# Banded attention and two gated layers on one core: the first unit's k and q at the head of the load queue, and the second batch's loads moved behind the first batch's units

## The chip, the core and the metric

The program runs on one core of one Trainium2 chip. The core has a matrix engine (PE, with its weight load PEld), a vector engine (DVE), an engine for activations and copies (ACT), a general engine (POOL) and an engine that only issues loads here (SP). The metric is the device time of one execution in microseconds, and of several executions the median.

## What is computed

Three steps in float32. First an attention over 2 batches, 8 heads, 768 positions and 64 columns a head, in which a position sees 31 neighbours and one summary row for each block of 32 positions:

```python
k_sum = k.reshape(B, H, nb, block, D).max(axis=3)
v_sum = v.reshape(B, H, nb, block, D).mean(axis=3)
scores_l = scale * np.matmul(q, k.transpose(0, 1, 3, 2))      # kept where |i - j| < 16
scores_s = scale * np.einsum('bhsd,bhnd->bhsn', q, k_sum) + np.log(block)
a = softmax(concatenate([scores_l_masked, scores_s], axis=-1))
x = np.matmul(a, np.concatenate([v, v_sum], axis=2))           # then (1536, 512)
```

Then two layers on the 1536 rows of x: `(sigmoid(x @ w_gate) * (x @ w_val)) @ w_out` with 1536 inner columns, and `max(x @ w1, x @ w2, x @ w3) @ w_out` with 768 inner columns.

## The kernel before

**Units.** The attention is cut into 16 units, one for a batch b, a pair of heads p (4 pairs) and a half of the positions a. The units run in the order b, a, p, so that units 0 to 7 are the first batch and 8 to 15 the second. `make_sums` makes, once for a batch and a pair, the block maxima of k (`ks`, on DVE, from the load `kn`) and the block means of v (`vs`; in the first batch eight matmuls on PE over the load `vn`, line 520; in the second three additions on POOL and one matmul). `make_unit` then makes a unit: scores on PE from q and k (line 590), mask and maximum on DVE (line 597), exponentials on ACT (line 603), division on DVE, transposes on PE (line 622), the product with v (line 632, the task kept in `pvs`), and the split of the result into a rounded part and a remainder (tile `x`; ACT line 348, DVE line 351). In the first batch the keys are read straight from `kn`; in the second batch each unit has a load of its own, `kw`. Each unit also loads `q` and `v`.

**Weights.** The weights arrive as 64-bit numbers, 512 KB for each 128x512 tile (`raw`, three buffers). DVE packs each into float32 in three passes (lines 405, 410 and 414), then ACT rounds it (line 348) and DVE takes the remainder (line 351) into `w`, of which there are twelve buffers. Every product is done as three matmuls of rounded parts. The first layer's products are at lines 711 and 745, the second's at 835 and 942.

**Order.** No order is written out. Every piece of work is a task with an engine, a duration, a due time and what it depends on, and `Plan.order` lays all tasks out by a list schedule with these figures. The instructions then stand in that order on each engine, and each engine works them off strictly in turn. So a load is not tied to its due time on the chip: it has a place in SP's queue, and SP issues it when its turn has come and its buffer is free. The argument `after` of a task only asks the plan to start it no sooner than another task has started; it adds no semaphore. While PE would wait early in the program, the plan fills the time with idle matmuls (line 994), as many as it expects to fit before the task's start, on the tile that the task will write.

The due times of loads are counted back from a unit's target T (`KEYS0`, `SUMS0`, `ROWS0` for the first batch; `KEYS`, `SUMS`, `ROWS` for the second) and from a weight's first use (`WLOAD`, and `WLOAD0` besides for the first ten weights). Of the loads that are ready, the one that is due first goes first.

Of the kernel before, what the change touches and what calls it, by code (L numbers as in the profile page):

```python
# [18 lines left out]
WIN = 16  # L19
# [8 lines left out]
LAST = 2  # L28
LASTACC = 12
KEYS0, KEYS = 14.0, 24.0  # L30
SUMS0, SUMS = 14.0, 8.0
ROWS0, ROWS = 2.0, 4.0
WLOAD = 24.0
WLOAD0 = 2.0
WREADY = 8.0
FREE_M = 2
BY_ACT = 6
# [6 lines left out]
BANKS_KW, BANKS_KN, BANKS_Q, BANKS_V = 2, 4, 3, 3  # L44
# [28 lines left out]
class Plan:  # L73
# [11 lines left out]
    def add(self, eng, dur, due, fn, deps=(), new=(), uses=(), after=(), tab=None):  # L85
        t = Task(eng, dur, due, fn, [d for d in deps if d], list(new), list(uses), [d for d in after if d], tab)
        self.tasks.append(t)
        return t
# [114 lines left out]
def kernel(  # L203
# [16 lines left out]
    B, NPAIR, _, S = qt.shape  # L220
    D = vw.shape[-1]
# [8 lines left out]
    TPU = HALF // 128  # L230
    CW = 96 + NB
# [55 lines left out]
    add = plan.add  # L287
# [5 lines left out]
    def psum_s(shape):  # L293
        return Buf(ps_s, shape, F32, "s", 4)
# [92 lines left out]
    def convert():  # L387
# [3 lines left out]
        def to_float(ck, t):  # L391
# [25 lines left out]
            n += 1  # L417
            l = add("SP", 1.456, t - WLOAD - WLOAD0 * (n <= 10), load, new=[r], after=[prev.get("l")])
            k1 = add("DVE", 0.335, t - 2.7, c1, [l], [c], [r], [prev.get("1")])
# [66 lines left out]
    def after(tag, t):  # L486

        p = chain.get(tag)
        if p:
            t.after.append(p)  # L490
        chain[tag] = t
        return t

    def load_task(tag, n, shape, src, dur, t):
        b = Buf(ap_, shape, F32, tag, n)

        def fn(what=tag):
            nc.sync.dma_start(out=b.t[0:src.shape[0]], in_=src)

        return b, after(tag, add("SP", dur, t, fn, new=[b]))  # L500

    kblock, vblock, pvs = {}, {}, {}
    attention = []

    def make_sums(b, p, T):

        kt, lk = load_task("kn", BANKS_KN, [128, S + 2 * WIN], kn[b, p], 1.14, T - (KEYS if b else KEYS0))
        r, lr = load_task("vn", 2, [96, 2, 8 * D], vn[b, p], 1.092, T - (SUMS if b else SUMS0))
        ks = Buf(ap_, [128, NB], F32, "ks", 4)
        vs = Buf(ap_, [128, 2 * D], F32, "vs", 4)  # L510
        ps = psum_s([128, 2 * D])

        def kmax():
            nc.vector.tensor_reduce(
                out=ks.t, in_=kt.t[:, WIN:WIN + S].rearrange("p (n w) -> p n w", w=BLK), axis=AX.X, op=ALU.max)

        def vsum():

            for n in range(8):
                nc.tensor.matmul(  # L520
                    ps.t, lhsT=avg, rhs=r.t[:, :, D * n:D * n + D], start=(n == 0), stop=(n == 7))

        def vadd():
            for n in (4, 2, 1):
                nc.gpsimd.tensor_tensor(
                    out=r.t[:, :, 0:n * D] if n > 1 else vr.t, in0=r.t[:, :, 0:n * D],
                    in1=r.t[:, :, n * D:2 * n * D], op=ALU.add)

        def vmean():
            nc.tensor.matmul(ps.t, lhsT=avg, rhs=vr.t, start=True, stop=True)  # L530

        def vcopy():
            nc.scalar.activation(out=vs.t, in_=ps.t, func=ACTF.Copy)

        k = add("DVE", 0.87, T - 13.5, kmax, [lk], [ks], [kt])
        if b == 0:
            v1, v2 = None, add("PE", 1.75, T - 5, vsum, [lr, built], [ps], [r])
        else:
            lr.after.append(pvs[4 + p])
            vr = Buf(ap_, [96, 2, D], F32, "vr", 2)  # L540
            v1 = add("POOL", 2.5, T - 8, vadd, [lr, built], [vr], [r])
            v2 = add("PE", 0.22, T - 5, vmean, [v1], [ps], [vr])
        v3 = add("ACT", 0.2, T - 4.5, vcopy, [v2], [vs], [ps])
        kblock[b, p] = ks, k, kt, lk
        vblock[b, p] = vs, v3
        attention.extend([k, v2, v3] + ([v1] if b else []))

    def make_unit(u, i):
        b, p, a = u
        T = target[u]  # L550
        if a == 0:
            make_sums(b, p, T)
        whole = b == 0
        ks, kk, kt, lk = kblock[b, p]
        if not whole:
            kt, lk = load_task("kw", BANKS_KW, [128, TPU, 2, CW], kw[b, p, a], 1.024, T - KEYS)
        q, lq = load_task("q", BANKS_Q, [128, HALF], qt[b, p, :, HALF * a:HALF * a + HALF], 0.546,
                          T - (KEYS0 if whole else KEYS))
        vt, lv = load_task("v", BANKS_V, [CW, TPU, 2, 2, D], vw[b, p, a], 0.82, T - (ROWS0 if whole else ROWS))
        vs, kv = vblock[b, p]  # L560
        e = [Buf(ap_, [128, TPU, CW], F32, f"e{h}", 2) for h in range(2)]
        nm = Buf(ap_, [128, 2, TPU], F32, "nm", 2)
# [395 lines left out]
    for i, u in enumerate(units):  # L958
        make_unit(u, i)
# [22 lines left out]
    with tc.manual_schedule():  # L982
        idle = const.tile([128, 384], BF16, name="idle")
        nc.vector.memset(idle, 0.0)
        for t in plan.order():
            for b in t.new:
                b.take()
            if t.idle:
# [3 lines left out]
                n = min(o.shape[1], 384)  # L992
# [62 lines left out]
```

## Time and profile before

| | |
|---|---|
| median of 3 runs | 565.29 us (564.71 to 569.85) |
| the profiled execution | 564.06 us, of which 562.3 us is the span from first to last instruction |
| PE busy | 543.9 us, 97% of the span |
| DVE busy | 430.7 us, 77% |
| ACT busy | 286.8 us, 51% |
| loads and stores | 71.96 MB, mean 128 GB/s over the span |

A busy PE is not PE at its peak, since its matmuls overlap and their ends are modelled. The shares are means over stages that differ: the attention of the first batch, the first layer with the second batch's attention beside it, the second layer, and the last product.

### The profile page before, as it was taken

To read this page: it belongs to the slowest core of one execution; us is meant where nothing else is said; L and a number is where in the kernel's file an instruction comes from. 1 tells how busy PE (TensorE), PEld (TensorE's weight loads), DVE (VectorE), ACT (ScalarE), POOL (GpSimd) and SP (SyncE) were. 2 spreads that over 40 slices of the span, in tenths; PEclk is the share of its full clock that TensorE was granted. 3 is DMA by queue.
4 is the path that set the end of the run, shared out by engine and by line. 5 is a ranking of instruction groups with operands and counts; after the bars stand their busy time and mean duration, and the time that the engine had idled before them with its cause. 6 is when DMAs were issued, how large, how long until landed. Compare 5 with 4: busy or idle time off the path is not lost.

```text
span 562.3 us, 10192 instructions
## 1 busy us (share of the span) xinstructions
PE 543.9 (97%) x3924; PEld 521.4 (93%) x3924; DVE 430.7 (77%) x987; ACT 286.8 (51%) x663; POOL 16.1 (3%) x30
## 2 busy tenths in 40 slices
PE   8689899999999999999999999999999999999997
PEld 7578799999999999999999999999999999997886
DVE  6789958894697598949996996799999997885000
ACT  4689776583765656966441332435344333453111
POOL 2001221100000000000000000000000000000000
PEclk9999999999999999999999999999999999999999
DMA  8999653563266453520652553120322222000111
GB/s 296 318 268 283 201 174 135 166 208 113 81 195 187 141 150 110 170 75 1 188 186 78 155 182 114 53 98 21 108 87 87 77 74 82 32 1 37 57 72 60
DMA packets 24288, 71.96 MB, mean 128 GB/s; under 512 B 2736, under 2 KB 6192, under 8 KB 24240
## 3 DMA queue, kind: packets, MB, share of 16 engines
q1 hardware_dynamic: 21120, 67.58, 38.7%
q10 hardware_dynamic: 3120, 3.74, 1.9%
q8 instruction: 31, 0.51, 0.4%
q14 instruction: 17, 0.14, 0.1%
HBM read 67.57 MB, written 3.15 MB: 126 GB/s over the span
## 4 chain that ended last, share of the span: by engine, by line
PE 81%; DVE 7%; DMA 5%; ACT 5%; issue 1%; SPq 1%; ACTq 0%; DVEq 0%
PE m L711 30%; PE m L745 16%; PE s L835 11%; PE m L835 11%; PE m L942 9%; DMA vn<-in_vn_dram 3%; PE s L632 2%; DMA raw<-in_wts_dram 1%; DVE c L414 1%; DVE c L410 1%; PE s L622 1%; ACT e L617 1%; ACT e L603 1%; DVE c L405 1%; PE s L590 1%
## 5 line engine op out<-in xcount | busy, mean ns | idle before, releaser
L711 PE MATMUL m<-x,w 128*128 128x384 f32 x1152 | 211.0, 338 | 0.5 <-ACT t L725 0.3
L711 PEld LDWEIGHTS m<-x,w 128*128 128x128 f32 x1152 | 198.7, 188 | 2.5 <-issue 0.6
L745 PE MATMUL m<-h,w 128*128 128x384 f32 x576 | 107.3, 338 | 0.7 <-DVE h L351 0.7
L745 PEld LDWEIGHTS m<-h,w 128*128 128x128 f32 x576 | 99.3, 188 | 2.0 <-DVE h L351 1.4
L348 ACT ACTIVATE w<-c 128x512 fp32r<-128x512 f32 x96 | 58.1, 610 | 71.6 <-DVE c L414 48.4
L351 DVE TENSOR_TENSOR w<-c,w 128x512 fp32r<-128x512 f32 x96 | 63.8, 665 | 12.6 <-ACT w L348 12.4
L414 DVE SCALAR_TENSOR_TENSOR c<-raw,c 128x512 int32<-128x512 int32 x96 | 66.7, 697 | 0.6
L410 DVE SCALAR_TENSOR_TENSOR c<-raw,c 128x512 int32<-128x512 int32 x96 | 66.0, 689 | 0.6
L835 PE MATMUL m<-x,w 128*128 128x384 f32 x294 | 56.3, 335 | 1.2 <-ACT t L850 1.2
L835 PE MATMUL s<-f,w 128*128 128x384 f32 x294 | 56.0, 334 | 0.0
L835 PEld LDWEIGHTS m<-x,w 128*128 128x128 f32 x294 | 51.3, 188 | 1.6 <-ACT t L850 1.5
L835 PEld LDWEIGHTS s<-f,w 128*128 128x128 f32 x294 | 51.4, 188 | 0.0
L405 DVE TENSOR_SCALAR c<-raw 128x512 int32<-128x512 int32 x96 | 41.7, 437 | 5.7 <-DMA raw<-in_wts_dram 4.7
L725 ACT ACTIVATE t<-m 128x384 f32<-128x384 f32 x48 | 23.4, 491 | 35.2 <-PE m L711 34.8
L730 DVE TENSOR_TENSOR t<-m,t 128x384 f32<-128x384 f32 x48 | 26.6, 554 | 15.3 <-PE m L711 10.8
L348 ACT ACTIVATE h<-t 128x384 fp32r<-128x384 f32 x48 | 24.9, 521 | 25.7 <-DVE t L730 23.8
L603 ACT ACTIVATE e<-e,nm 128x120 f32<-128x120 f32 x96 | 36.6, 384 | 1.3 <-DVE nm L597 1.1
L351 DVE TENSOR_TENSOR h<-t,h 128x384 fp32r<-128x384 f32 x48 | 26.9, 563 | 5.4 <-ACT h L348 5.4
L952 ACT ACTIVATE c<-m 128x512 f32<-128x512 f32 (+1 forms) x13 | 7.3, 565 | 40.0 <-PE m L942 39.6
L850 ACT ACTIVATE t<-s 128x384 f32<-128x384 f32 x27 | 13.3, 491 | 24.4 <-PE s L835 24.4
L942 PE MATMUL m<-w,x 128*128 128x512 f32 (+1 forms) x126 | 24.9, 359 | 0.0
L942 PE MATMUL m<-w,f 128*128 128x512 f32 x108 | 24.7, 389 | 0.0
(108 smaller groups left out, 586.4 us busy)
## 6 DMA issues: line engine op xcount, KB each, us to landing
raw<-in_wts_dram SPq DMA_DIRECT2D x96, 512.0 KB, 4.3
v<-in_vw_dram SPq DMA_DIRECT2D x16, 288.0 KB, 4.8
kn<-in_kn_dram SPq DMA_DIRECT2D x8, 400.0 KB
vn<-in_vn_dram SPq DMA_DIRECT2D x8, 384.0 KB
q<-in_qt_dram SPq DMA_DIRECT2D x16, 192.0 KB, 5.2
kw<-in_kw_dram SPq DMA_DIRECT2D x8, 360.0 KB, 10.0
out_dram<-c ACTq DMA_DIRECT2D x11, 256.0 KB, 2.0
v<-vs ACTq DMA_DIRECT2D x8, 72.0 KB
```

Of the source, the lines that this page charges most:

```text
L348: nc.scalar.activation(out=dst, in_=src, func=ACTF.Copy)
L351: nc.vector.tensor_tensor(out=dst, in0=src, in1=h.bitcast(F32), op=ALU.subtract)
L405: nc.vector.tensor_scalar(out=c.t, in0=half(r, 1), scalar1=5, scalar2=2, op0=ALU.logical_shift_left, op1=ALU.logical_shift_right)
L410: nc.vector.scalar_tensor_tensor(out=c.t, in0=half(r, 1), scalar=-0x40000000, in1=c.t, op0=ALU.bitwise_and, op1=ALU.bitwise_or)
L414: nc.vector.scalar_tensor_tensor(out=c.t, in0=half(r, 0), scalar=29, in1=c.t, op0=ALU.logical_shift_right, op1=ALU.bitwise_or)
L603: nc.scalar.activation(out=e[h].t[:, t], in_=e[h].t[:, t], func=ACTF.Exp, scale=-1.0, bias=nm.t[:, h, t:t + 1], accum_out=sm.t[:, h, t:t + 1])
L711: nc.tensor.matmul(ps.t, lhsT=w.t.rearrange("p s (k f) -> p s k f", k=KC)[:, wh, kc], rhs=src[kc // 2].t[:, xh, kc % 2], start=(kc == 0 an ...
L725: k1 = after("t", add("ACT", 0.371, end, lambda: nc.scalar.activation(out=s.t, in_=ps.t, func=ACTF.Sigmoid), [l], [s], [ps], tab="S"))
L730: k2 = after("t", add("DVE", 0.469, end, lambda: nc.vector.tensor_tensor(out=t.t, in0=ps2.t, in1=s.t, op=ALU.mult), [l2, k1], [t], [ps2, s]))
L745: nc.tensor.matmul(ps.t, lhsT=w.t.rearrange("p s (k f) -> p s k f", k=KC)[:, wh, dm], rhs=h.t[:, xh], start=(i == 0 and j == 0), stop=(i = ...
L835: nc.tensor.matmul(ps.t, lhsT=w.t[:, wh, c:c + 128], rhs=x.t[:, xh, kc], start=new and n == 0, stop=n == 5, skip_group_check=True)
L942: nc.tensor.matmul(ps.t[:, c0:c1], lhsT=h.t[:, xh, e, c:c + 128], rhs=w.t[:, wh, c0:c1], start=(f == 0 and i == 0), stop=(f == NF2 - 1 and ...
```

## The change

Three things are changed. `SUMS0` goes from 14 to 12 and `WLOAD0` from 2 to -1, which moves the due times of the first batch's loads for the means and of the first ten weights later against those of k and q. And `load_task` takes a list `held`: each load of the second batch, except `vn`, which had such an entry before, gets an `after` on the task `pvs` of the unit four places earlier (for `kn` the unit `NPAIR + p`).

```diff
-SUMS0, SUMS = 14.0, 8.0
+SUMS0, SUMS = 12.0, 8.0
 ROWS0, ROWS = 2.0, 4.0
 WLOAD = 24.0
-WLOAD0 = 2.0
+WLOAD0 = -1.0
...
-    def load_task(tag, n, shape, src, dur, t):
+    def load_task(tag, n, shape, src, dur, t, held=()):
...
-        return b, after(tag, add("SP", dur, t, fn, new=[b]))
+        return b, after(tag, add("SP", dur, t, fn, new=[b], after=held))
...
-        kt, lk = load_task("kn", BANKS_KN, [128, S + 2 * WIN], kn[b, p], 1.14, T - (KEYS if b else KEYS0))
+        kt, lk = load_task("kn", BANKS_KN, [128, S + 2 * WIN], kn[b, p], 1.14, T - (KEYS if b else KEYS0), [pvs[NPAIR + p]] if b else [])
...
+        held = [] if whole else [pvs[i - NPAIR]]
         if not whole:
-            kt, lk = load_task("kw", BANKS_KW, [128, TPU, 2, CW], kw[b, p, a], 1.024, T - KEYS)
+            kt, lk = load_task("kw", BANKS_KW, [128, TPU, 2, CW], kw[b, p, a], 1.024, T - KEYS, held)
         q, lq = load_task("q", BANKS_Q, [128, HALF], qt[b, p, :, HALF * a:HALF * a + HALF], 0.546,
-                          T - (KEYS0 if whole else KEYS))
-        vt, lv = load_task("v", BANKS_V, [CW, TPU, 2, 2, D], vw[b, p, a], 0.82, T - (ROWS0 if whole else ROWS))
+                          T - (KEYS0 if whole else KEYS), held)
+        vt, lv = load_task("v", BANKS_V, [CW, TPU, 2, 2, D], vw[b, p, a], 0.82, T - (ROWS0 if whole else ROWS), held)
```

Since the plan then lays everything out anew, the order changes on every engine until about line 745's third group of products; from there on PE's order is the same in both. Four places follow. In them `in_wts_dram`, `in_kn_dram`, `in_vn_dram`, `in_qt_dram`, `in_vw_dram` and `in_kw_dram` are the inputs behind `raw`, `kn`, `vn`, `q`, `v` and `kw`.

SP's queue from its first load on, lines with a minus only before, with a plus only after:

```order
+L498 DMA kn<-in_kn_dram 128x800
+L498 DMA q<-in_qt_dram 128x384
 L398 DMA raw<-in_wts_dram 128x1024
-L498 DMA kn<-in_kn_dram 128x800
 L498 DMA vn<-in_vn_dram 96x1024
-L498 DMA q<-in_qt_dram 128x384
 L398 DMA raw<-in_wts_dram 128x1024 x2
 L498 DMA kn<-in_kn_dram 128x800
+L498 DMA q<-in_qt_dram 128x384
 L498 DMA vn<-in_vn_dram 96x1024
-L498 DMA q<-in_qt_dram 128x384
```

The first k and q now stand ahead of the first weight, and the second q ahead of the second `vn`; the set of the first fourteen loads is the same in both.

SP's queue from its fifteenth load on:

```order
-L398 DMA raw<-in_wts_dram 128x1024
 L498 DMA v<-in_vw_dram 96x768
-L498 DMA kw<-in_kw_dram 128x720
-L498 DMA vn<-in_vn_dram 96x1024
-L498 DMA kw<-in_kw_dram 128x720
 L398 DMA raw<-in_wts_dram 128x1024
 L498 DMA q<-in_qt_dram 128x384
 L498 DMA vn<-in_vn_dram 96x1024
+L398 DMA raw<-in_wts_dram 128x1024
 L498 DMA q<-in_qt_dram 128x384
+L498 DMA vn<-in_vn_dram 96x1024
+L498 DMA v<-in_vw_dram 96x768
```

Two loads of `kw`, for units 8 and 9, are gone from here. They come back at places 36 and 45 of the queue (17 and 19 before); the second batch's four `kn` go from places 32, 36, 44 and 50 to 35, 44, 50 and 55.

DVE from its second instruction on, before (a row with `e_221` is the mask and maximum of unit 0):

```order
L405 TENSOR_SCALAR c<-raw 128x512
L410 SCALAR_TENSOR_TENSOR c<-raw,c 128x512
L514 TENSOR_REDUCE ks<-kn 128x24
L414 SCALAR_TENSOR_TENSOR c<-raw,c 128x512
L351 TENSOR_TENSOR w<-c,w 128x512
L405 TENSOR_SCALAR c<-raw 128x512
L410 SCALAR_TENSOR_TENSOR c<-raw,c 128x512
L414 SCALAR_TENSOR_TENSOR c<-raw,c 128x512
L405 TENSOR_SCALAR c<-raw 128x512
L597 ISA e_221,nm<-s,masks 128x120
```

The same place after:

```order
L514 TENSOR_REDUCE ks<-kn 128x24
L405 TENSOR_SCALAR c<-raw 128x512
L410 SCALAR_TENSOR_TENSOR c<-raw,c 128x512
L414 SCALAR_TENSOR_TENSOR c<-raw,c 128x512
L351 TENSOR_TENSOR w<-c,w 128x512
L599 ISA e_139,nm<-s,masks 128x120
```

The block maximum moves ahead of the first weight, and one weight instead of two and a part stands ahead of unit 0's mask and maximum.

PE at its first useful instructions, before, from the last of the first 48 idle matmuls to the first of the 27 that follow:

```order
L994 MATMUL s<-idle 128x128
L520 MATMUL s<-vn,avg 128x128 x8
L590 MATMUL s<-kn,q 64x96 x12
L590 MATMUL s<-ks,q 64x24 x12
L994 LDWEIGHTS idle
```

And after, from the last of all ten idle matmuls:

```order
L996 MATMUL s<-idle 128x360
L592 MATMUL s<-kn,q 64x96 x12
L592 MATMUL s<-ks,q 64x24 x12
L520 MATMUL s<-vn,avg 128x128 x8
L592 MATMUL s<-kn,q 64x96 x12
```

Unit 0's scores move ahead of the first means. Of 78 idle matmuls, 75 with 128 columns and three with 384, ten with 360 columns are left, all of them at the very start. On ACT the loads of a function table go from 22 to 24.

## Rows read from the trace of the kernel before

**Rows 1.** Busy time and instructions of each engine by stretch, clock, DMA share, GB/s.

```profile
0.00:10.00 10.00, 8.17 (x112) 7.81 (x112) 4.79 (x9) 2.69 (x4) 3.92 (x18) 1.00 0.82 285
10.00:20.00 10.00, 7.86 (x180) 7.00 (x174) 8.08 (x37) 7.17 (x29) 0.00 (x0) 1.00 1.04 333
20.00:30.00 10.00, 6.49 (x103) 5.41 (x102) 8.50 (x33) 6.89 (x23) 0.00 (x0) 1.00 1.05 294
30.00:40.00 10.00, 8.68 (x127) 7.48 (x120) 8.54 (x35) 7.80 (x24) 0.00 (x0) 1.00 1.02 262
40.00:50.00 10.00, 9.40 (x130) 8.22 (x131) 9.96 (x36) 9.90 (x25) 0.00 (x0) 1.00 0.87 275
60.00:70.00 10.00, 9.45 (x116) 8.72 (x117) 9.97 (x41) 8.36 (x26) 1.46 (x2) 1.00 0.75 236
70.00:80.00 10.00, 9.98 (x93) 8.72 (x92) 5.99 (x12) 7.19 (x27) 3.52 (x4) 1.00 0.72 216
...
240.00:490.00 250.00, 250.00 (x1464) 249.60 (x1463) 218.09 (x410) 103.64 (x195) 0.00 (x0) 1.00 0.31 95
```

**Rows 2.** Waits of DVE in 0 to 62 us: total, times, longest.

```profile
DVE c L405 <- DMA raw<-in_wts_dram: 4.7, 3, 3.3
DVE ks L514 <- DMA kn<-in_kn_dram: 1.9, 2, 1.3
```

**Rows 3.** DVE in order of time, 0 to 46 us: start, us, instruction, [idle before].

```profile
4.44 0.43 DVE L405 TENSOR_SCALAR c<-raw 128x512 int32<-128x512 int32 x1 [3.31 <-DMA raw<-in_wts_dram]
...
5.72 0.95 DVE L514 TENSOR_REDUCE ks<-kn 128x24 f32<-128x768 f32 x1
...
7.97 0.69 DVE L351 TENSOR_TENSOR w<-c,w 128x512 fp32r<-128x512 f32 x1 [0.70 <-ACT w L348]
...
10.86 0.28 DVE L597 CUSTOM_DVE_ANT_0 e<-s,masks 128x120 f32<-128x120 f32 x1
...
16.89 0.95 DVE L514 TENSOR_REDUCE ks<-kn 128x24 f32<-128x768 f32 x1 [1.25 <-DMA kn<-in_kn_dram]
...
19.66 0.95 DVE L514 TENSOR_REDUCE ks<-kn 128x24 f32<-128x768 f32 x1 [0.60 <-DMA kn<-in_kn_dram]
...
28.30 0.56 DVE L351 TENSOR_TENSOR x<-s,x 128x384 fp32r<-128x384 f32 x1 [1.10 <-ACT x L348]
...
34.19 0.43 DVE L405 TENSOR_SCALAR c<-raw 128x512 int32<-128x512 int32 x1 [0.51 <-DMA raw<-in_wts_dram]
...
38.28 0.43 DVE L405 TENSOR_SCALAR c<-raw 128x512 int32<-128x512 int32 x1 [0.85 <-DMA raw<-in_wts_dram]
```

**Rows 4.** Loads by source: count, KB each, median us from issue to landing.

```profile
raw<-in_wts_dram SPq DMA_DIRECT2D x96, 512.0 KB, 4.3
...
kn<-in_kn_dram SPq DMA_DIRECT2D x8, 400.0 KB
vn<-in_vn_dram SPq DMA_DIRECT2D x8, 384.0 KB
q<-in_qt_dram SPq DMA_DIRECT2D x16, 192.0 KB, 5.2
kw<-in_kw_dram SPq DMA_DIRECT2D x8, 360.0 KB, 10.0
```

**Rows 5.** SP, PE and ACT in order of time, 0 to 30 us.

```profile
0.80 1.28 ACT L348 ACT_TABLE_LOAD   x1 [0.80 <-PEq L1040]
...
1.19 5.30 PE L994 MATMUL s<-idle 128*128 128x128 bf16 x48 [1.19 <-DVE idle L984]
...
7.14 2.02 PE L520 MATMUL s<-vn,avg 96*128 96x128 f32 x16 [0.64 <-DMA vn<-in_vn_dram]
...
9.09 0.72 PE L590 MATMUL s<-kn,q 64*64 64x96 f32 x24
...
10.06 1.68 PE L994 MATMUL s<-idle 128*128 128x128 bf16 x27
...
24.83 2.05 PE L520 MATMUL s<-vn,avg 96*128 96x128 f32 x16 [1.07 <-DMA vn<-in_vn_dram]
```

## The prediction, before the changed kernel was run

> **What bounds the kernel now.** I read the table of stretches first. From 240 to 490 us PE is busy 250.00 of 250 us, and already in 60 to 80 us it is busy 9.45 and 9.98 of 10 [rows 1]. So from about 62 us on the matrix engine sets the end. What is queued there must be done whatever the loads do, and PE's order in the last three quarters of the program is not changed. A gain can only come from reaching that point sooner; this is the first thing the reader is to see, since it caps everything below.
>
> Before that point PE is not the bound. From 40 us DVE is: 9.96 of 10 busy, and 9.97 in 60 to 70 [rows 1]. From 10 to 40 us it is 8.08, 8.50 and 8.54, while the DMA share is 1.04, 1.05 and 1.02: all sixteen DMA engines are working all the time. So the start has two bounds, the loads and then DVE, and DVE's idle time up to 40 us is what a better order of loads can give back. It is 5.21 + 1.92 + 1.50 + 1.46 = 10.1 us, of which some 4.1 cannot go, because nothing can be worked on before the first load has landed. The cap is thus 6 us, about 1% of the run.
>
> The waits of DVE say whose fault that idle time is: 4.7 us for weights, 1.9 us for k [rows 2]. In order of time [rows 3] these are 3.31 us for the first weight, then 1.25 and 0.60 us for the third and fourth `kn`, 1.10 us at 28.30 for a result of unit 1, and 0.51 and 0.85 us for the sixth and seventh weight.
>
> **The head of the queue.** With k first, 400 KB land ahead of where 512 KB landed at 4.44 us; at the 285 GB/s of the first stretch [rows 1, 4] the missing 112 KB are 0.4 us, so k is there at 4.1 us. q is then there after 592 KB, at 4.7. Unit 0's scores stood at 9.09 us behind the first means, which began at 7.14 [rows 5]; now they can start at 4.7, 4.4 us sooner. That is the visible effect and most of it is lost at once. On DVE the unit's mask and maximum still stands behind the whole first weight. That weight now lands behind k and q, after 1,104 KB. Before, 912 KB had landed by 5.72 (block maximum) and 1,296 KB by 7.14 (first means), so 1,104 KB lie half way, at 6.4 us. From its first pass at 4.44 to the end of its remainder at 8.66 DVE took 4.2 us with the block maximum (0.95) in between [rows 3], so 3.3 without; 6.4 + 3.3 = 9.7 us against 10.86 us before. The lead is 1.2 us, not 4.4.
>
> And the lead ends at the next load. The third `kn`, for which DVE waited until 16.89, has the same ten loads ahead of it as before; so does the fourth with its thirteen. With the DMA engines full, moving loads among themselves moves no landing of the last of them. DVE comes to the third block maximum up to 1.2 us sooner and waits that much longer. I count the head of the queue at **0**; bounds are a gain of 1.2 us, if the third `kn` comes with the lead, and a loss of 1.0 us, the extra wait for the first weight (3.31 us before, now 3.0 for k and 6.4 - 5.0 = 1.4 for the weight).
>
> **The two `kw` loads taken out of the early queue.** These are 720 KB that no unit needs before the first batch is done. What stood behind them comes sooner. The third `vn` is the eighteenth load in both queues, but with one q where a `kw` was: 168 KB less, at 299 GB/s between 20 and 30 us some 0.5 us. PE waited for it until 24.83 [rows 5], unit 1's product with v stood behind it, and that made the 1.10 us wait at 28.30. **Gain 0.5.** The sixth weight has 528 KB less ahead of it (two `kw` out, one q in), the seventh 720 KB; at 294 and 262 GB/s, mean 278, they come 1.9 and 2.6 us sooner. The waits were 0.51 and 0.85, so both go. **Gain 1.4.** What is late next is DVE itself, at 9.96 of 10, and beside it ACT with 9.90 in 40 to 50 us: nothing more is to be had there. In the order of the changed kernel DVE has nearly the same weights and the same units ahead of each result of units 2 to 5, so the 1.9 us should be carried on to 62 us.
>
> **What is put back.** The `kw` and `kn` of the second batch come after 40 us, where the DMA share is 0.87 and then 0.75 [rows 1]; two `kw` and one `kn` are 1.1 MB, over 40 us 28 GB/s more on 236 to 275, under the 333 that the early stretch reached. They stand behind loads of v that wait for a unit's product, and some weights stand behind them. But weights then wait for buffers that PE frees, so I count 0. If that cover fails, the closest case is the third `kn` of the second batch, at place 50: it is issued right behind a weight that waits for DVE, three to four DVE operations before its block maximum, and a landing takes 4.3 us for a weight, so DVE could stand for 1 to 2 us near 70 us. In 70 to 80 us DVE is busy only 5.99 of 10, so even this would hardly reach PE. The two more table loads on ACT are 2 x 1.28 = 2.6 us [rows 5]; ACT is at 8.36 and 7.19 of 10 in 60 to 80 us, which holds them. Bounds: 0 and a loss of 2.6.
>
> **The idle matmuls.** The first 48 took 5.30 us, 110 ns for 128 columns, and the 27 at 10.06 us took 1.68, or 62 ns [rows 5]. That is the step between 1.2 and 2.4 GHz, although the column of the granted clock shows 1.00 throughout [rows 1]; before it lay five microseconds without a gap. Now 10 x 360 columns at the lower rate are about 3.1 us, then a pause until q is there. So PE may take the step later. Up to 24 us its useful work is roughly 7 us from 10 to 20 us less the 1.7 of idle matmuls, and 3 more around it: 9 us at most, which at the lower rate (x1.77) grows by 7 us. PE had 2.1 and 3.5 us free in 10 to 30 us, and what it delivers is awaited by a DVE that waits for loads anyway. I count 0, bounded by a loss of 3 us.
>
> The Trainium skill, "TensorE: Matmul & The Clock Gate", section "Part 1: The HAM clock gate", says that the throttled state is the default and that activity releases it. By that rule taking out 68 idle matmuls speaks against this change; the 110 and 62 ns agree with it. By the rule alone this term would be at its bound of 3 us, and the sum a loss of 1.1; carried further it is the third rival below.
>
> **Sum.** 0 - 0.5 - 1.4 + 0 + 0 = -1.9 us, from a span of 562.3 to 560.4. The profiled execution was 564.06 us, 1.8 us outside the span; so 562.2. The median of the runs before, 565.29, is 1.2 above the profiled one, and times are compared with it: I say **563.2 us**. About 1% (5.7 us) is what a measurement of this kernel can tell from no change, its three runs lying 5.1 us apart.
>
> **Rivals.** (1) *Loads hidden anyway*, 565.3: the sixth and seventh weight come sooner but DVE's next operation in turn is then held by ACT, which is full from 40 us, and the 28.30 wait is replaced by another on the same result. For it: all of DVE's work ahead of unit 2's scores is the same. Against: both waits for weights name the DMA and nothing else.
> (2) *The loads move as a whole*, 560: the third and fourth `kn` also come sooner, since two `kw` no longer share the engines while these are in flight. Then the 1.9 us for k, the other 0.6 of the 1.10 and the 0.7 ahead of the first remainder [rows 3] are saved besides: 1.9 + 1.9 + 0.6 + 0.7 = 5.1 us, and more than 1% only if nearly all of the cap of 6 us comes. For it: by 16.89 us the engines had moved 285 x 10 + 333 x 6.9, or 5.1 MB, while the first eleven loads are 3.9 MB and one v [rows 4], so later loads had a share in the time. Against: a share that q and weights in the same places would take as well.
> (3) *The clock*, 571 to 575: PE stays at 1.2 GHz past unit 2's scores, near 24 us. From there PE is the bound of the start. Its busy time from 10 to 50 us is 32.4 us, less 1.7 idle; at x1.77 it grows by 23.6 us, of which 7.6 are free now; 16 us are left, and since PE then works without a gap I take half to three quarters of them, 8 to 12, less the gain of 1.9. If it ends before 24 us, it costs nothing to 3 us.
> (4) *The wait in the queue*, 567.7: the held v at place 47 waits for unit 5's product, and the weights behind it come late. Price: one landing of a weight on which DVE waits, 4.3 us [rows 4], less the gain. It decides if DVE has used up its three weight buffers before that product is done; DVE's 5.99 of 10 in 70 to 80 us speaks against it.
>
> **Chances.** The forecast 0.50, (1) 0.20, (2) 0.15, (3) 0.07, (4) 0.08. From these: faster by over 1% (under 559.6) 0.11, from the upper part of (2) and the tail of the forecast; within 1% 0.82; slower by over 1% 0.07. The range takes in forecast, (1), (4) and most of (2): 559.0 to 568.0.
>
> **What would show it.** Right: scores of unit 0 near 4.7 us, its maximum near 9.7, third and fourth block maximum still near 16.5 and 19.5 with waits for `kn`, no wait for a weight between 30 and 40 us, PE busy without gaps from about 60 us, DMA share above 0.8 in 40 to 70 us. Wrong: the third block maximum at 15 us or before; matmuls of 128x384 at twice their time after 20 us; new waits of PE or DVE for `kn`, `kw` or `v` after 60 us; or a second half that is not as long as before.

## The result and the profile after

The changed kernel took 570.99 us in the median (570.24 to 573.20, 8 runs); beside it the kernel before took 564.74 us. The ratio is 1.0108, 95% interval 1.0086 to 1.0130: it is slower by 1.1%, about 6 us. In all that follows, runs more than 1.5% above the fastest of their kernel (one of e14's ten) are left out of ratios and spreads. The profiled execution was 570.24 us with a span of 568.5, 6.2 us more than before.

First the table of stretches of the changed kernel, with the same columns as [rows 1]: busy us and instructions of PE, PEld, DVE, ACT and POOL, then granted clock, DMA share and GB/s.

```profile
0.00:10.00 10.00, 5.14 (x62) 3.27 (x63) 2.98 (x5) 1.85 (x2) 3.68 (x18) 0.88 0.78 244
10.00:20.00 10.00, 8.79 (x104) 8.28 (x104) 8.48 (x38) 6.25 (x25) 0.00 (x0) 0.61 1.05 284
20.00:30.00 10.00, 5.05 (x75) 4.05 (x72) 8.00 (x30) 5.91 (x24) 0.00 (x0) 0.74 1.04 266
30.00:40.00 10.00, 9.77 (x150) 8.98 (x152) 5.73 (x25) 6.64 (x21) 0.00 (x0) 0.75 0.63 187
40.00:50.00 10.00, 9.16 (x151) 8.00 (x142) 9.49 (x34) 9.80 (x25) 0.00 (x0) 1.00 0.62 184
60.00:70.00 10.00, 8.43 (x109) 7.47 (x108) 8.27 (x24) 6.27 (x16) 2.54 (x3) 1.00 0.64 199
70.00:80.00 10.00, 9.21 (x63) 8.57 (x64) 9.02 (x29) 8.39 (x24) 2.83 (x3) 0.83 0.89 306
...
240.00:490.00 250.00, 250.00 (x1465) 249.61 (x1463) 218.04 (x416) 107.50 (x208) 0.00 (x0) 1.00 0.32 97
```

The last line is that of before: 250 of 250 us and one matmul more. The loss lies ahead of it, and three columns show it. The DMA share in the first 30 us is as full as before, but the bytes are fewer: 244, 284 and 266 GB/s for 285, 333 and 294. The granted clock, 1.00 throughout before, is 0.61 to 0.75 from 10 to 40 us. And from 60 to 70 us DVE, which was at 9.97, has 1.7 us without work; PE, which was at 9.45 and 9.98 from 60 to 80 us, is at 8.43 and 9.21.

How late PE is can be counted. These are the same view, from 0 to 200 us, of the matmuls of the first layer alone (x by w, then h by w), before:

```profile
0.00:200.00 200.00, 98.61 (x518) 88.95 (x519) 1.00 0.63 196
0.00:200.00 200.00, 46.33 (x240) 41.13 (x240) 1.00 0.63 196
```

and after:

```profile
0.00:200.00 200.00, 92.17 (x488) 83.79 (x489) 0.94 0.64 194
0.00:200.00 200.00, 47.66 (x240) 42.52 (x240) 0.94 0.64 194
```

PE has done 30 matmuls fewer. Where it is always busy it does one in 250 / 1464 = 0.171 us, so 5.1 of the 6.2 us are lost by then.

DVE after, in order of time (start, us, instruction, idle before it), the lines that answer to [rows 3]:

```profile
3.92 0.95 DVE L514 TENSOR_REDUCE ks<-kn 128x24 f32<-128x768 f32 x1 [2.78 <-DMA kn<-in_kn_dram]
7.52 0.43 DVE L405 TENSOR_SCALAR c<-raw 128x512 int32<-128x512 int32 x1 [2.65 <-DMA raw<-in_wts_dram]
...
10.71 0.28 DVE L599 CUSTOM_DVE_ANT_0 e<-s,masks 128x120 f32<-128x120 f32 x1
...
17.61 0.95 DVE L514 TENSOR_REDUCE ks<-kn 128x24 f32<-128x768 f32 x1 [1.29 <-DMA kn<-in_kn_dram]
...
22.21 0.95 DVE L514 TENSOR_REDUCE ks<-kn 128x24 f32<-128x768 f32 x1 [1.83 <-DMA kn<-in_kn_dram]
...
33.79 0.56 DVE L351 TENSOR_TENSOR x<-s,x 128x384 fp32r<-128x384 f32 x1 [3.61 <-ACT x L348]
...
63.33 0.53 DVE L405 TENSOR_SCALAR c<-raw 128x512 int32<-128x512 int32 x1 [1.73 <-DMA raw<-in_wts_dram]
```

k is there early, as meant. The first weight comes at 7.52 us, the third and fourth block maximum start 0.7 and 2.6 us later than before, and unit 1's remainder 5.5 us later, at 33.79. No weight is waited for between 30 and 40 us any more; at 63 us there is a wait of 1.73 us that before did not have.

PE after, in order of time, for [rows 5]:

```profile
1.20 3.17 PE L996 MATMUL s<-idle 128*128 128x360 bf16 x10 [1.20 <-DVE idle L986]
4.53 0.72 PE L592 MATMUL s<-kn,q 64*64 64x96 f32 x24 [0.16 <-DMA q<-in_qt_dram]
9.06 3.75 PE L520 MATMUL s<-vn,avg 96*128 96x128 f32 x16 [3.50 <-DMA vn<-in_vn_dram]
...
27.99 3.75 PE L520 MATMUL s<-vn,avg 96*128 96x128 f32 x16 [1.33 <-DMA vn<-in_vn_dram]
31.67 1.55 PE L634 MATMUL s<-at,v 120*64 120x64 f32 x24
...
70.09 0.44 PE L747 MATMUL m<-h,w 128*128 128x384 f32 x1 [1.09 <-ACT h L348]
71.23 2.85 PE L747 MATMUL m<-h,w 128*128 128x384 f32 x11 [0.70 <-DVE h L351]
```

Unit 0's scores start at 4.53 us and take 0.72, as before. Then PE waits 3.50 us for `vn`, and the means behind that wait take 3.75 us, for 2.02 and 2.05 before: the lower clock. The third means come at 27.99 for 24.83, again at the lower clock. At 70 and 71 us PE, which was to be busy from 60 us on, waits for the second step's input.

SP's queue after, in order of time: the loads that stand ahead of the weight for which DVE waits at 63 us.

```profile
45.27 6.98 SPq L398 DMA_DIRECT2D raw<-in_wts_dram  x3
52.30 0.42 SPq L498 DMA_DIRECT2D kn<-in_kn_dram  x1
52.78 0.42 SPq L498 DMA_DIRECT2D kw<-in_kw_dram  x1
53.25 0.43 SPq L498 DMA_DIRECT2D q<-in_qt_dram  x1
53.79 0.37 SPq L498 DMA_DIRECT2D v<-in_vw_dram  x1
54.21 0.44 SPq L498 DMA_DIRECT2D vn<-in_vn_dram  x1
56.69 0.95 SPq L398 DMA_DIRECT2D raw<-in_wts_dram  x2
```

Three weights go out one by one until 52 us, as DVE frees their buffers; then five loads of the second batch, 1,624 KB, go out in two microseconds, and the next weight behind them. What the weights waited for, from 44 to 58 us (total, times, longest):

```profile
SPq L398 <- DVE c L414: 4.2, 2, 2.2
SPq L398 <- DVE c L405: 3.0, 1, 3.0
```

### The profile page after: what moved, and what is told of

It reads as the page before. It is cut to its first block, busy times and chain, and to the rows that moved or that the text cites. A ratio compares the mean times of both kernels' runs of the same rounds, so it can differ in the third digit from the quotient of the medians.

```text
span 568.5 us, 10061 instructions
## 1 busy us (share of the span) xinstructions
PE 546.6 (96%) x3856; PEld 524.0 (92%) x3856; DVE 428.7 (75%) x987; ACT 289.7 (51%) x665; POOL 14.6 (3%) x30
## 4 chain that ended last, share of the span: by engine, by line
PE 77%; DMA 8%; DVE 7%; ACT 6%; issue 1%; SPq 1%; ACTq 0%; DVEq 0%
PE m L713 27%; PE m L747 16%; PE s L837 11%; PE m L837 11%; PE m L944 9%; DMA raw<-in_wts_dram 3%; DMA vn<-in_vn_dram 2%; DMA q<-in_qt_dram 2%; PE s L634 1%; ACT e L605 1%; DVE c L414 1%; DVE c L410 1%; PE s L592 1%; DVE w L351 1%; DVE c L405 1%
## 5 line engine op out<-in xcount | busy, mean ns | idle before, releaser
L747 PE MATMUL m<-h,w 128*128 128x384 f32 x576 | 108.6, 341 | 1.8 <-ACT h L348 1.1
L747 PEld LDWEIGHTS m<-h,w 128*128 128x128 f32 x576 | 100.6, 190 | 2.9 <-ACT h L348 1.4
L405 DVE TENSOR_SCALAR c<-raw 128x512 int32<-128x512 int32 x96 | 40.2, 423 | 6.8 <-DMA raw<-in_wts_dram 5.8
```

The lines of the kernel that those rows point to most:

```text
L405: nc.vector.tensor_scalar(out=c.t, in0=half(r, 1), scalar1=5, scalar2=2, op0=ALU.logical_shift_left, op1=ALU.logical_shift_right)
L747: nc.tensor.matmul(ps.t, lhsT=w.t.rearrange("p s (k f) -> p s k f", k=KC)[:, wh, dm], rhs=h.t[:, xh], start=(i == 0 and j == 0), stop=(i = ...
```

## Experiments

Three theories stood after the result: the order of the first loads (head), the block of held loads ahead of a weight (block), and the clock that PE loses where the 68 idle matmuls are gone (clock). Ratios are to the kernel before, run beside it on the same chip; 1% is 5.7 us.

**e1: the head alone.** The kernel before with the two new numbers; the plan then lays out everything anew, with the ten idle matmuls.

```diff
-SUMS0, SUMS = 14.0, 8.0
+SUMS0, SUMS = 12.0, 8.0
...
-WLOAD0 = 2.0
+WLOAD0 = -1.0
```

> Only SUMS0 12 and WLOAD0 -1; nothing held. PE's order has the ten idle matmuls of the changed kernel at the start and none later, and the two early kw stay in the queue. Theory A (PE at its lower clock delays the first units): PE shows 0.50 in some stretches before 36 us as in the changed kernel, and the time is most of the changed kernel's loss, 568 to 571 us. Theory B (the held loads, which then come in a block ahead of weights 12 to 15 and make DVE and PE wait at 60 to 72 us): no such waits, 564 to 566 us.

571.53 us (570.73 to 573.47), ratio 1.0112 (1.0084 to 1.0139): by itself it costs as much as the whole change. GB/s are 222 and 279 in the first two stretches, the clock 0.50 from 10 to 20 us, and the fourth block maximum starts at 23.51. Head and clock come together here, so the number alone does not tell them apart.

**e2: the held loads alone.** The changed kernel with the two old numbers.

```diff
-SUMS0, SUMS = 12.0, 8.0
+SUMS0, SUMS = 14.0, 8.0
...
-WLOAD0 = -1.0
+WLOAD0 = 2.0
```

> Only the holding of the second batch's loads; SUMS0 14 and WLOAD0 2 as before, so that weight, kn, vn, q head the queue and 77 idle matmuls stay. Theory A: granted clock 1.00 throughout, gain from the early queue without kw as I forecast, 562 to 565 us. Theory B: the block of held loads still stands ahead of weights 12 to 15, waits of DVE for a weight and of PE at 60 to 72 us, 567 to 570 us.

568.55 us (567.35 to 570.16), ratio 1.0050 (1.0024 to 1.0076). The start is that of before, 285 and 330 GB/s with 77 idle matmuls, and the fourth block maximum at 19.86. But DVE waits for a weight at 60 us, and PE at 67. And the clock did not stay up, as the first theory had it: it is 0.66 from 20 to 30 us, the third means take 3.78 us, and DVE then waits 3.02 us for ACT, which waits for transposes of PE that stand behind these means. In order of time, DVE and then PE of this run:

```profile
30.39 0.17 DVE L610 TENSOR_SCALAR sm<-sm 128x3 f32<-128x3 f32 x1 [3.02 <-ACT e L605]
...
60.11 0.54 DVE L405 TENSOR_SCALAR c<-raw 128x512 int32<-128x512 int32 x1 [2.78 <-DMA raw<-in_wts_dram]
...
24.27 3.78 PE L520 MATMUL s<-vn,avg 96*128 96x128 f32 x16 [1.44 <-DMA vn<-in_vn_dram]
...
67.41 0.69 PE L747 MATMUL m<-h,w 128*128 128x384 f32 x1 [1.39 <-ACT h L348]
```

**e3: idle matmuls put back.** The changed kernel with 70 more, ahead of four of PE's early tasks.

```diff
+        fill = {2: 28, 3: 4, 11: 18, 13: 20}
+        npe = -1
         for t in plan.order():
             for b in t.new:
                 b.take()
+            if t.eng == "PE":
+                npe += 1
+                t.idle += fill.get(npe, 0)
```

> The changed kernel in its own order, with 70 idle matmuls more at the four places where PE waited in its trace: 28 ahead of the first means, 4 ahead of unit 1's scores, 18 ahead of unit 1's transposes, 20 ahead of the third means. Theory A: granted clock 1.00 from about 8 us on, third vn and the products with v earlier by 2 to 4 us, 565 to 568 us. Theory B: the clock rises but the time stays, 569 to 572 us.

569.31 us (567.30 to 572.02), ratio 1.0074 (1.0046 to 1.0102), so 1.9 us back of 6.1 by the medians; the interval overlaps that of the whole change (1.0086 to 1.0130), so this is not clear of noise. The clock is 1.00, 0.84, 0.99 and 1.00 by tens of microseconds, the loads are as late as in the changed kernel: third and fourth block maximum at 19.41 and 23.32.

**e4: idle matmuls taken from before.** Only the first 28 of 78 are left.

```diff
+        left = 28
         for t in plan.order():
             for b in t.new:
                 b.take()
+            t.idle = min(t.idle, left)
+            left -= t.idle
             if t.idle:
```

> The kernel before in its own order, with the first 28 of its 78 idle matmuls only (3.1 us of them, as long as the changed kernel's ten). Theory A: PE at the lower clock in some stretch before 36 us and 567 to 570 us. Theory B: lower clock or not, within 1 us of before, 564 to 566 us.

564.42 us (562.16 to 565.95, 10 runs), ratio 0.9982 (0.9965 to 0.9999). The clock fell to 0.50 from 20 to 30 us and was 0.86 behind it, and nothing was lost, although unit 1's remainder came 3.3 us later than before:

```profile
31.63 0.56 DVE L351 TENSOR_TENSOR x<-s,x 128x384 fp32r<-128x384 f32 x1 [3.50 <-ACT x L348]
```

In before's order a low clock by itself costs nothing: what is late at 30 us was made up later, and the waits of 0.51 and 0.85 us for the sixth and seventh weight are gone.

**e5: the new head alone, all else as before.** The first nine loads exchange places; PE, DVE, ACT and POOL keep the order of before.

```diff
+        order = plan.order()
+        slots = [i for i, t in enumerate(order) if t.eng == "SP"][:9]
+        left = [order[i] for i in slots]
+        for i, tag in zip(slots, ("kn", "q", "raw", "vn", "raw", "raw", "kn", "q", "vn")):
+            t = next(t for t in left if t.new[0].tag == tag)
+            left.remove(t)
+            order[i] = t
-        for t in plan.order():
+        for t in order:
```

> The kernel before, every engine in its own order, 78 idle matmuls as before; only SP's first nine loads stand as in the changed kernel (kn, q, raw, vn, raw, raw, kn, q, vn). Theory C (the new head makes the DMA engines move fewer bytes while they are busy, so that all later loads land late): third and fourth block maximum start after 18 and 22 us instead of 16.9 and 19.7, under 300 GB/s in 10 to 20 us, time 567 to 570 us. Rival D (the landings are late only because the changed kernel's other engines are late): 16.9 and 19.7 as before, 330 GB/s, 565 to 567 us from the later first weight alone.

570.08 us (566.99 to 571.99), ratio 1.0076 (1.0046 to 1.0107). The table of stretches:

```profile
0.00:10.00 10.00, 5.26 (x53) 5.12 (x54) 2.80 (x5) 1.33 (x2) 3.69 (x18) 0.88 0.79 254
10.00:20.00 10.00, 10.00 (x128) 9.60 (x131) 8.05 (x27) 5.11 (x18) 0.00 (x0) 0.61 1.05 283
```

The same nine loads move fewer bytes at the same DMA share, and the third and fourth block maximum start late, for 16.89 and 19.66 before:

```profile
19.34 0.94 DVE L514 TENSOR_REDUCE ks<-kn 128x24 f32<-128x768 f32 x1
...
21.75 0.95 DVE L514 TENSOR_REDUCE ks<-kn 128x24 f32<-128x768 f32 x1
```

DVE here still has the first weight ahead of the first block maximum and stands until 7.30 us (4.44 before); the changed kernel has the maximum in this gap, so the cost need not be the same there. PE waits for `vn` and loses its clock too, with all 78 idle matmuls in place.

**e6: the old head in the changed kernel.** The snippet of e5 with the tags raw, kn, vn, q, raw, raw, kn, vn, q.

> The changed kernel, every engine in its order, only SP's first nine loads stand as before (raw, kn, vn, q, raw, raw, kn, vn, q). Theory C: third and fourth block maximum back at 16.9 and 19.7 us, over 320 GB/s in 10 to 20 us, and 567 to 569 us; what is left of the loss is the block of held loads and the clock. Rival D: no gain, 570 to 572 us.

568.63 us (566.19 to 569.51), ratio 1.0048 (1.0025 to 1.0071); 283 and 324 GB/s, third and fourth block maximum at 15.40 and 18.40. The loads are in time again and the clock is not (0.61 and 0.73 from 10 to 30 us), and the wait for the weight at 61.55 (2.43 us) is still there.

**e7: the two early `kw` alone.** In the kernel before, these two loads move back from places 17 and 19 of the queue to 36 and 45.

```diff
+        order = plan.order()
+        early = [t for t in order if t.eng == "SP" and t.new[0].tag == "kw"][:2]
+        order = [t for t in order if t not in early]
+        for t, n in zip(early, (34, 43)):
+            sp = [i for i, u in enumerate(order) if u.eng == "SP"]
+            order.insert(sp[n] + 1, t)
-        for t in plan.order():
+        for t in order:
```

> The kernel before, every engine in its order; only the two kw loads at places 17 and 19 of SP's queue are moved to places 36 and 45. My term for them: the sixth and seventh weight and the third vn land sooner, the waits of 0.51, 0.85 and part of 1.10 us go, 563.5 us (1.9 less). Rival: DVE's other work and ACT take the place of these waits, 565 to 566 us.

563.77 us (562.03 to 568.17, 12 runs), ratio 0.9974 (0.9956 to 0.9993): 1.5 us faster. The waits for the sixth and seventh weight are 0.20 us together for 1.36, and the one ahead of unit 1's remainder 0.72 for 1.10.

**e8: the block moved.** The kernel of e2 with `kn`, `kw`, `q` and `vn` of the second batch's first pair behind the next two weights.

```diff
+        order = plan.order()
+        sp = [t for t in order if t.eng == "SP"]
+        i = next(i for i, t in enumerate(sp) if t.new[0].tag == "kw")
+        block = [t for t in sp[i - 1:i + 4] if t.new[0].tag != "v"]
+        raws = [t for t in sp[i:] if t.new[0].tag == "raw"][:2]
+        order = [t for t in order if t not in block]
+        at = order.index(raws[1]) + 1
+        order[at:at] = block
-        for t in plan.order():
+        for t in order:
```

> The kernel with only the holding of the second batch's loads, every engine in its order; in the first block of held loads kn, kw, q and vn are moved behind the next two weights. Theory B (the block of 1.6 MB ahead of the twelfth weight makes DVE wait for it, 2.78 us at 60 us in that kernel's trace, and PE at 67 us): no such wait of DVE, 566 to 567 us, 2 less than with the block. Rival: DVE's wait is only moved to the block maximum of the second batch or PE has work in hand, 568 to 569 us.

565.35 us (564.49 to 567.17, 12 runs), ratio 1.0000 (0.9985 to 1.0014): against e2 that is 0.50%, 2.8 us. Of the gain by the early `kw` (e7) nothing is left here: the third means are slow as in e2 (3.64 us), and DVE waits 2.65 us at 30 us. The wait for the weight at 60 us is gone. From 60 to 70 us, first e2, then e8:

```profile
60.00:70.00 10.00, 7.28 (x94) 5.91 (x92) 9.85 (x32) 6.82 (x18) 1.95 (x3) 0.87 0.64 210
```
```profile
60.00:70.00 10.00, 9.78 (x118) 8.84 (x117) 9.96 (x41) 9.63 (x28) 2.98 (x3) 1.00 0.96 281
```

PE is busy 9.78 for 7.28 us. What is late next is a wait of PE for DVE's remainder at 78.41 us (2.06).

**e9: all three taken out.** The changed kernel with the edits of e3, e6 and e8 together.

> The changed kernel with the three suspected costs taken out together: the first nine loads in the order of before, the second batch's first kn, kw, q and vn behind the next two weights, and seventy idle matmuls put back ahead of PE's early tasks. Nothing is left of the change but the later kw loads and the order that the plan then gives the engines. Theory A (the loss of about 6 us is the head of the queue, the block ahead of weight 12 and the clock, and nothing else; the later kw are then worth 1 to 2 us as they were alone): 563 to 566 us, no wait of DVE for a weight near 60 us, third and fourth block maximum before 17.2 and 20.0. Theory B (the new order on PE, DVE and ACT has a cost of its own): 567 us or more with all three out.

561.49 us (561.01 to 562.07, 6 runs), ratio 0.9922 (0.9895 to 0.9949): 4.4 us faster than before, and better than either theory had it. The stretches:

```profile
0.00:10.00 10.00, 5.62 (x65) 3.73 (x66) 4.06 (x11) 2.07 (x3) 3.70 (x18) 1.00 0.82 293
10.00:20.00 10.00, 10.00 (x171) 9.35 (x171) 8.52 (x36) 7.46 (x31) 0.00 (x0) 1.00 1.04 333
20.00:30.00 10.00, 9.73 (x168) 8.12 (x160) 8.63 (x39) 6.26 (x21) 0.00 (x0) 1.00 1.03 265
```

The bytes of before in the first 20 us, and the full clock. By 200 us the first layer has 535 + 240 matmuls done for 518 + 240 before, 17 x 0.171 = 2.9 us, against 3.0 us less span. So the loss was in these three things; whatever else the plan laid out anew comes, taken together, to a gain.

**e10, e11: k ahead in other orders.** The kernel before, by the snippet of e5, with kn, raw, vn, q, raw, raw, kn, vn, q and with kn, raw, q, vn, raw, kn, raw, q, vn.

> The kernel before with one exchange in the load queue: the first kn ahead of the first weight, q and all else where they were. Theory A (the DMA engines move fewer bytes where the first weight, vn and two more weights, all with rows of 4,096 bytes, stand in one row with no load of shorter rows between): that row is broken by q here, so 280 and 320 GB/s or more in the first two stretches of ten microseconds, third and fourth block maximum before 17.4 and 20.2, 564 to 567 us. Theory B (k ahead of the first weight is enough): 254 and 283 GB/s as with the whole new head, third block maximum after 18.5, 568.5 us or more.

> The kernel before with its first nine loads as kn, raw, q, vn, raw, kn, raw, q, vn: k first, and a load of shorter rows behind every one or two of the loads with rows of 4,096 bytes. Theory A (a row of long-row loads lowers the rate): 285 and 325 GB/s or more in the first two stretches, third block maximum before 17.4, 564 to 567 us. Theory B (k ahead of the first weight is enough): 255 and 285 GB/s, third block maximum after 18.5, 568.5 us or more.

567.84 us, ratio 1.0035 (1.0012 to 1.0059), 277 and 288 GB/s; and 566.53 us, ratio 1.0016 (0.9993 to 1.0040), 263 and 290 GB/s. In both the fourth block maximum is late (20.49, 20.96), the third a little (17.47, 17.72). The row of long loads is not the reason, since both orders break it and the second stretch stays low. But neither is as slow as the whole new head.

**e12, e13: the weight in front, and `vn` in front.** The orders raw, kn, q, vn, raw, raw, kn, q, vn and vn, raw, kn, q, raw, raw, kn, vn, q.

> The kernel before with its first nine loads as raw, kn, q, vn, raw, raw, kn, q, vn: the first weight stays in front and only q and vn are exchanged, twice. Theory B (what lowers the rate is that k stands ahead of the first weight, since all three orders that had it so gave 283 to 290 GB/s from 10 to 20 us and all that had the weight in front 324 to 333): 320 GB/s or more from 10 to 20 us, third and fourth block maximum before 17.3 and 20.2, 564 to 567 us. Theory C (it is q ahead of vn that puts the long loads side by side): 285 GB/s, third block maximum after 18, 567.5 us or more.

> The kernel before with its first nine loads as vn, raw, kn, q, raw, raw, kn, vn, q: one load of 384 KB in front of the first weight that is not k. Theory B (the rate hangs on the first weight being the first load): 283 to 290 GB/s from 10 to 20 us as with k in front, third block maximum after 17.4, 567 us or more. Theory B2 (it is k in front, not any other load): 320 GB/s or more, third block maximum before 17.3; the first weight lands about 1 us late all the same, 565 to 567 us.

565.89 us, ratio 1.0041 (1.0023 to 1.0059), 272 and 309 GB/s, fourth block maximum at 20.00; and 565.12 us, ratio 1.0019 (0.9997 to 1.0040), 304 and 280 GB/s, at 20.34. The first falls between its two theories; the second has the rate of the one and the time of the other: over 20 us both moved 5.8 MB, where before moved 6.2 and the kernels with the new head 4.8 to 5.4. Each rate is that of one execution. No single load explains the rate, and which property of an order does stays open.

**e14: loads right, few idle matmuls.** e9 without the 70 idle matmuls.

> The changed kernel with the head of the queue as before and the second batch's first kn, kw, q and vn behind the next two weights, and the ten idle matmuls that its own plan gave it. Beside the same kernel with seventy idle matmuls more (561.5 us) it shows what the clock costs once both load orders are put right. Theory A (the low clock costs where PE's results are awaited; it cost 1.7 us in the changed kernel): a granted clock under 0.8 in one of the stretches from 10 to 30 us and 562.5 to 564.5 us. Theory B (with the loads in time DVE waits for loads and not for PE, so the clock costs nothing, as in the kernel before with 28 idle matmuls): 561 to 562.3 us at the same low clock.

566.10 us (562.43 to 568.86 and one at 572.12, 10 runs), ratio 1.0020 (0.9991 to 1.0049). More than either theory had: beside e9 the 70 idle matmuls are worth 0.98%, 5.5 us. The clock is 0.83 from 20 to 30 us; the profiled run has means of 3.78 and 3.22 us at 9.52 and 16.84. Unit 1's remainder, first here and then in e9:

```profile
30.12 0.56 DVE L351 TENSOR_TENSOR x<-s,x 128x384 fp32r<-128x384 f32 x1 [3.16 <-ACT x L348]
```
```profile
28.47 0.56 DVE L351 TENSOR_TENSOR x<-s,x 128x384 fp32r<-128x384 f32 x1 [0.80 <-ACT x L348]
```

That this wait is where the time goes is not shown: e4 had a longer one at the same place and lost nothing. The runs are 6.4 us apart, those of e9 1.1; but with all 78 idle matmuls those of e7 are 6.1 apart.

**e15: the new head with the clock kept up.** e5 with 36 more idle matmuls ahead of PE's first task.

```diff
+        order[next(i for i, t in enumerate(order) if t.eng == "PE")].idle += 36
```

> The kernel before with the new order of its first nine loads, and 36 idle matmuls more ahead of the first means, so that PE does not pause for the later vn and its clock stays up. Theory A (the new head costs by its bytes, that is by loads that land later): 568.5 us or more at a clock of 0.95 or above from 10 to 20 us, third and fourth block maximum as late as 18.5 and 21.5. Theory B (the new head costs by the clock, which PE loses while it waits for vn; the late loads are made up): 567 us or less.

569.82 us (568.21 to 571.21), ratio 1.0060 (1.0035 to 1.0085), at a clock of 0.83 from 10 to 20 us and 1.00 elsewhere up to 80 us; the clock was not quite kept (0.95 was expected), but e5 had 0.61. Third and fourth block maximum start at 19.68 and 22.73. So most of the head's cost, 3.4 of e5's 4.3 us, is there although most of the clock is kept. The two runs cannot be told apart by their intervals, and the loads of this run came later still (231 and 268 GB/s), so the clock's share in the head is not measured.

**e16: the head left in.** e9 with the new head.

> The changed kernel with the new head kept, the second batch's first kn, kw, q and vn behind the next two weights and the seventy idle matmuls. Between the run with all three out (0.9922 of before) and the run with the idle matmuls alone (1.0074) it shares out the 8.6 us between head and block. Theory A (both cost, about as much as alone): 564.5 to 567.5 us. Theory B (the block is all of it once the clock is up): 561 to 563 us. Theory C (the head is all of it): 568 us or more.

566.99 us (564.33 to 569.08, 10 runs), ratio 1.0021 (0.9995 to 1.0046). From e3 to here the block gives back 0.53%, 3.0 us; from here to e9 the head gives back 0.99%, 5.6 us. The first step is at the edge of the noise, and the second has some clock in it (0.66 from 10 to 20 us here, 1.00 in e9). Both cost, as the first theory had it.

## Why the prediction was wrong

Forecast were 563.2 us and a range up to 568.0; measured were 570.99. Three terms that were counted at zero cost 2 to 4 us each, and the one gain came. By their own single runs: `kw` -1.5 (e7), head +4.3 (e5), block +2.8 (e2 less e8), clock +1.9 (e3), together 7.5 against 6.1 measured; they were measured in different orders of work and need not add up. The sum has a slip: 562.2 and 1.2 make 563.4, not 563.2, and nothing hangs on it.

**The head: the step that failed first.** "With the DMA engines full, moving loads among themselves moves no landing of the last of them" supposed that full engines move the same bytes. They did not: at much the same share the first two stretches moved 244 and 284 GB/s for 285 and 333. [rows 1] held the warning: at shares of 1.04, 1.05 and 1.02 before moved 333, 294 and 262. Hence the first weight came at 7.5 us and not 6.4, unit 0's maximum at 10.71 and not 9.7, and the third and fourth `kn` did not keep their times but came 0.7 and 2.6 us late. The bound on the losing side, 1.0 us, counted only the first weight; the term measured 4.3 us in before's order (e5), and 3.4 (e6) to 5.6 us (e16 and e9) in the changed one.

**The two `kw`.** Right as a mechanism and nearly in size: -1.9 forecast, -1.5 measured alone (e7), with the waits of 0.51 and 0.85 us gone as foreseen. Only the half microsecond for the third `vn` did not come in the changed kernel, where the slower head moved that load from 24.83 to 27.99.

**What is put back: the second step that failed.** The cover named was that "weights then wait for buffers that PE frees", and the closest case was placed at the third `kn`, near 70 us, at 1 to 2 us. The weights did wait for buffers, but for those of `raw`, which DVE frees (SP stood 4.2 and 3.0 us for them). So the block came out behind three weights at 52 us, all at once, and the next weight behind it was needed at once by the very engine that had held it up. 1,624 KB then stood before a weight that DVE needed: issued at 56.69, it was worked on at 63.33, 6.6 us for the 4.3 of [rows 4]. It hurt because DVE was at its limit there, and PE was hit 7 us later. The fourth rival came nearest: a weight on which DVE waits lands late behind held loads, priced at 4.3 us, measured 2.8, with a chance of 0.08. Its cause was another: there a v was to wait for a product, but the v of this block went out at 53.79 right behind the q, and what stood ahead of the weight were the bytes.

**The idle matmuls.** The term stood at 0 with a bound of 3, on the argument that what PE delivers late is awaited by a DVE that waits for loads anyway. In the changed kernel that argument is nearly right: 1.9 us, not clear of noise (e3). With the loads in time the same matmuls are worth 5.5 us (e14 and e9), beyond the bound. So by the medians the losses hide one another, and taking out one gives back little: 1.9 us for the clock alone, 3.4 for the old head alone (e6), 5.0 for both loads (e14), but 10.5 for all three. The third rival's time of 571 to 575 was all but met in number, by luck: the clock was low past 24 us again, but not without pause, and alone it gave back the least of the three.

The Trainium skill, "TensorE: Matmul & The Clock Gate", section "Part 1: The HAM clock gate", has the throttled state as the default and activity as what releases it. The trace agrees: ten idle matmuls and one set of scores, a pause of 3.5 us, and the means behind it at 3.75 us for 2.05. But whether that costs time was a matter of the order: nothing in before's (e4), 5.5 us in the changed one with its loads in time. Which wait makes the difference is not shown.

**What was not foreseen at all** is the gain that e9 shows, 4.4 us where the two `kw` account for 1.5. The rest, 2.9 us, came with the new order on the engines, the other held loads and the new places of the idle matmuls, which no run took apart; the held loads with the two old numbers and without the block gained nothing (e8). The rival that loads "move as a whole" had put such a gain at 560, by another way.

**What would show it.** Right: scores at 4.53 us, no wait for a weight from 30 to 40. Wrong, and each of them a sign of one of the three: first weight 7.5 and maximum 10.7 (head), DMA share 0.62 from 40 to 50 and 0.64 from 60 to 70 us and a wait of DVE for a weight at 63 (block), slow matmuls after 20 us (clock).

## What to carry to other kernels

A load queue whose engines are full is not a pipe of fixed rate: when loads change places, look at the bytes moved in the stretch after. Here the fourth `kn` came 2.6 us late. A load that is held back lands somewhere; find the place in the queue where the held ones come out together, and ask which weight stands right behind them and whether its consumer is at its limit there. When two limits of a start overlap, an experiment that lifts one shows only the difference between them, so lift them together before a term is called small.

## What the runs showed of the hardware

**DMA.** At a share of 1.04 to 1.05 of the sixteen engines the second ten microseconds moved from 268 GB/s (e15) to 333 (before, e9), for the most part by the order of the first nine loads. With k first it was 268 to 290 in all eight kernels, with the first weight and the old order behind it 312 to 333 in all of e2, e4, e6 to e9 and e14; q ahead of `vn` gave 309, close to the lowest of these, `vn` first 280. It is not the mix of loads: in the first 20 us before moved 6.19 MB in 2205 packets and the changed kernel 5.28 MB in 1914, 2.8 KB each in both. Packets of one size took longer: in these 20 us those of 4,096 bytes 189 ns in the mean before and 217 after, those of 3,200 bytes 143 and 172. Why is not settled. The changed kernel in steps of two microseconds (time, PE busy, clock, DMA share, GB/s) shows that it is not even within an order:

```profile
8.00:10.00 2.00, 0.94 (x4) 0.50 1.00 363
...
12.00:14.00 2.00, 0.82 (x4) 0.50 1.09 251
```

Both lines have full engines, and one moves 45% more than the other.

**The clock.** In these lines the granted clock is 0.50, the lower of two levels, 1.2 of 2.4 GHz. Before it lay ten idle matmuls up to 4.4 us, the scores, still at the speed of before, and a pause of 3.5 us. At that level the sixteen means took 3.75 us for 2.05, a unit's product with v 1.55 for 0.92. The column of the clock is coarse: in e14 it says 1.00 from 10 to 20 us, where the means take 3.78 and 3.22 us, so durations of one shape are the better reading.
